# One weight load held for 1200 matmuls: the ones of a column sum kept in TensorE

## The chip, the cores and the metric

The kernel runs on one core of a Trainium2 chip. The metric is the device time of one execution in microseconds (us). The median of several is quoted. Single executions of one kernel here lie within about 0.4% (3 us) of each other, so differences under 1 us are read from several rounds and from the traces together. The engines are TensorE (matmuls; PE in the profile), VectorE (DVE), ScalarE (ACT), GpSimd (POOL) and SyncE (SP), which here issues the transfers. DMA engines, 16 of them, carry the transfers. A load *lands* when the last of them has reported its part.

## The reference, cut to what matters

```
x: (1, 384, 384, 384) bf16,  w1d: (1,) bf16
g = sum of x over the 384 x 384 positions, per channel, / (384 * 384)
s = sigmoid(g * w1d[0])                 # 384 numbers
return x * s                            # every position scaled by its channel
```

x has 113 MB. All of it must be summed before any of it can be scaled, and the kernels here keep only part of it on the chip, so most of it is read twice and all of it is written once: the page before has 190.41 MB read and 113.25 MB written.

## The kernel before

The 147456 positions are 1152 rows of 128 partitions x 384 channels. An arena on the chip holds 275 rows. In a first stage every row is read and summed by TensorE. Some rows stay in the arena for the second stage, and groups of them are squeezed by VectorE and ScalarE (`bits`, `join`, `test`: a fourth row is hidden in the spare bits of three others). In the second stage rows are scaled and stored, and the rest is read again.

The sum is a matmul with a 128 x 128 matrix of ones as weights and a row as moving data; all of them add into one bank `acc`:

```
def load(chunk, a, lo, hi):                       # one DMA from the queue of SyncE
    nc.sync.dma_start(out=arena[:, a : a + hi - lo, :], in_=view(xf, r0, n)[:, lo:hi, :])

def sum_rows(a, n):
    for i in range(a, a + n):                     # 1152 times in all
        nc.tensor.matmul(acc, lhsT=ones[:], rhs=arena[:, i, :], start=first, stop=last)   # L241

def keep_warm(n):                                 # 3 x 16 times, adds nothing
    nc.tensor.matmul(acc, lhsT=zeros[:], rhs=<ones, 384 columns>, start=False, stop=False)  # L256
...
# the last loads of the first stage: 13, 8, 13, 13, 8, 8, 5 and 3 rows
for a, n in S2 + [(U, 8)] + S3 + S1 + [(V, 8), (Y, 8), (T, 5), (T + 5, 3)]:
    take_raw(a, n)                                # load, then sum_rows
nc.scalar.activation(out=s_bf[:], in_=acc, func=ACTF.Sigmoid, scale=w_sc[:, 0:1])
...
# second stage: scale (VectorE), store and load (SyncE)
```

Each `matmul` becomes two instructions of TensorE, a weight load (LDWEIGHTS, in the profile "PEld") and the matmul proper ("PE").

Of the kernel before, what the change touches and what calls it, by code (L numbers as in the profile page):

```python
# [127 lines left out]
def kernel(  # L128
# [11 lines left out]
    nc = tc.nc  # L140
    P = nc.NUM_PARTITIONS
    B, H, W, C = x.shape
# [40 lines left out]
    ones = pool.tile([P, P], bf16, name="ones")  # L183
# [4 lines left out]
    arena = pool.tile([P, ROWS, C], bf16, name="arena")  # L188
    s_bf = pool.tile([P, C], bf16, name="s_bf")
    zeros = pool.tile([P, P], bf16, name="zeros")  # L190
    seen = pool.tile([P, 2 * len(pieces)], f32, name="seen")
    odd_i = pool.tile([P, 1], mybir.dt.int32, name="odd_i")
    bank0 = psum.tile([P, nc.PSUM_BANK_SIZE_BYTES // 4], f32, name="bank0")
    acc, votes = bank0[:, 0:C], bank0[:, C : C + 1]
# [12 lines left out]
    fl = Flow(nc, tc)  # L207
# [22 lines left out]
    def load(chunk, a, lo, hi):  # L230
# [5 lines left out]
            writes=rows(a, hi - lo), dma=True,  # L236
        )

    def sum_rows(a, n):
        def emit(i, first, last):  # L240
            return nc.tensor.matmul(acc, lhsT=ones[:], rhs=arena[:, i, :], start=first, stop=last)  # L241

        for i in range(a, a + n):
            first, last = summed[0] == 0, summed[0] == RPP - 1
            fl.add(
                "PE", lambda i=i, f=first, l=last: emit(i, f, l),
                reads=[("a", i), "ones"], writes=["bank0"],
            )
            summed[0] += 1

    def keep_warm(n):

        for _ in range(n):
            fl.add(
                "PE",
                lambda: nc.tensor.matmul(  # L256
                    acc, lhsT=zeros[:], rhs=ones[:, None, :].to_broadcast([P, C // P, P]), start=False, stop=False
                ),
                reads=["zeros", "ones"], writes=["bank0"],
            )  # L260

    def bits(dst, src, op0, s0, op1, s1, reads, writes):
        fl.add(
# [17 lines left out]
    def fold(k):  # L281
# [46 lines left out]
        reads=["ones", "w_bf"], writes=["bank0"],  # L328
# [4 lines left out]
        reads=["bank0"], writes=["w_sc"],  # L333
# [6 lines left out]
    def stream(n, a):  # L340
        load(STREAMED, a, streamed[0], streamed[0] + n)
        if n > 40 and folding:
            keep_warm(N_WARM)
        sum_rows(a, n)
        streamed[0] += n
# [11 lines left out]
    def take(g, lo=0, hi=None):  # L357

        a, q = GROUPS[g]
        hi = 4 * q if hi is None else hi  # L360
        load(KEPT, a + lo, c_group[g] + lo, c_group[g] + hi)
        sum_rows(a + lo, hi - lo)
# [36 lines left out]
    first = N_STREAM - between  # L399
# [22 lines left out]
    def take_raw(a, n):  # L422
        load(KEPT, a, raw(a), raw(a) + n)
        sum_rows(a, n)

    for a, n in S2 + [(U, 8)] + S3 + S1 + [(V, 8), (Y, 8), (T, 5), (T + 5, 3)]:
# [6 lines left out]
        reads=["bank0", "w_sc"], writes=["s_bf"],  # L433
# [231 lines left out]
    while True:  # L665

        if dve_at <= now:
# [4 lines left out]
            if landed and (ahead < PENDING or not can):  # L672
# [4 lines left out]
                if end or ahead < MERGE:  # L677
                    b, first = since
# [88 lines left out]
```

## Time and profile before

| kernel before | |
|---|---|
| median of the first 3 runs | 723.45 us |
| span of the profiled run | 721.3 us |
| TensorE | 1202 weight loads, 1202 matmuls, all but one in the first 270 us |
| landing of the last 8-row load that TensorE waits for | 266.50 us |

Three more lines of the page matter later: the first is from the part on busy time (engine, busy us, share, instructions), the others from the part on DMA queues (queue, kind: packets, MB, share of 16 engines).

```profile
PE 214.6 (30%) x1202; PEld 119.2 (17%) x1202; DVE 496.3 (69%) x470; ACT 115.4 (16%) x92; POOL 0.2 (0%) x4
...
q8 instruction: 9, 0.15, 0.1%
q14 instruction: 7, 0.06, 0.0%
```

Besides the data, the DMA engines fetch the engines' instructions: 9 packets on q8 and 7 on q14. By number, q8 is TensorE's. 9 packets of 16384 B over TensorE's 2404 instructions are 61 B for each (an estimate).

The timeline around 48 us (start us, us, engine, line, operation, count) shows how loads and matmuls lie:

```profile
47.83 1.46 PE L241 MATMUL bank<-arena,ones 128*128 128x384 bf16 x8
48.00 1.07 PEld L241 LDWEIGHTS bank<-arena,ones 128*128 128x128 bf16 x7
```

Seven loads lie inside eight matmuls that follow one another without a gap.

### The profile page before, as it was taken

What the parts mean: (1) busy time and instruction counts of PE and PEld (TensorE: products, weight loads), DVE (VectorE), ACT (ScalarE), POOL (GpSimd) and SP (SyncE); (2) the same over time, 40 slices, a digit from 0 to 9 for tenths busy, and PEclk for the clock granted to TensorE, in tenths of its full rate; (3) what the DMA queues carried; (4) which work ended last, traced back from release to release, by engine and by line L of the source; (5) the groups of instructions that cost most, each with busy time, mean ns of one, the idle gap of its engine ahead of it and who ended that gap; (6) DMA issues with size and microseconds to landing.
All of it is one profiled execution on the core that took longest, in us unless ns stands there. A gap on an engine that the chain in (4) does not pass through costs nothing.

```text
span 721.3 us, 3240 instructions
## 1 busy us (share of the span) xinstructions
PE 214.6 (30%) x1202; PEld 119.2 (17%) x1202; DVE 496.3 (69%) x470; ACT 115.4 (16%) x92; POOL 0.2 (0%) x4
## 2 busy tenths in 40 slices
PE   4677788897987770000000000000000000000000
PEld 2344445554543430000000000000000000000000
DVE  4600004788899819989799999999996992558500
ACT  3600003566677610002000000000000000000000
POOL 0000000000000000000000000000000000000000
PEclk9799999999899995555555555555555555555555
DMA  9999999999999978999999999999999999999997
GB/s 382 429 443 424 425 435 430 431 433 433 424 427 427 428 320 341 425 430 426 403 430 436 428 438 430 429 439 433 432 432 439 423 445 431 432 430 433 435 436 306
DMA packets 18882, 303.87 MB, mean 421 GB/s; under 512 B 2098, under 2 KB 2098, under 8 KB 4658
## 3 DMA queue, kind: packets, MB, share of 16 engines
q1 hardware_dynamic: 18864, 303.67, 98.6%
q8 instruction: 9, 0.15, 0.1%
q14 instruction: 7, 0.06, 0.0%
q10 hardware_dynamic: 2, 0.00, 0.0%
HBM read 190.41 MB, written 113.25 MB: 421 GB/s over the span
## 4 chain that ended last, share of the span: by engine, by line
DMA 55%; DVE 28%; PE 6%; ACT 5%; SPq 0%; issue 0%; another core or an unknown queue 0%; DVEq 0%
DMA arena<-in_x_dram 38%; DVE arena L441 19%; DMA out_dram<-arena 17%; DVE arena L265 6%; PE bank L241 6%; ACT arena L302 5%; DVE arena L271 3%; SPq L235 0%; ACT s_bf L432 0%; SPq L762 0%; DVEq L112 0%; SPq L106 0%
## 5 line engine op out<-in xcount | busy, mean ns | idle before, releaser
L441 DVE TENSOR_TENSOR arena<-arena,s_bf 128x1536 bf16<-128x1536 bf16 (+8 forms) x103 | 242.3, 2391 | 59.0 <-DMA arena<-in_x_dram 42.0
L265 DVE TENSOR_SCALAR arena<-arena 128x1536 uint16<-128x1536 uint16 (+2 forms) x247 | 145.5, 634 | 113.4 <-DMA arena<-in_x_dram 100.8
L241 PE MATMUL bank<-arena,ones 128*128 128x384 bf16 x1152 | 206.5, 341 | 52.7 <-DMA arena<-in_x_dram 52.6
L241 PEld LDWEIGHTS bank<-arena,ones 128*128 128x128 bf16 x1152 | 114.3, 102 | 144.6 <-DMA arena<-in_x_dram 58.7
L271 DVE TENSOR_TENSOR arena<-arena 128x1536 uint16<-128x1536 uint16 (+2 forms) x114 | 121.2, 1063 | 6.7 <-PE bank L241 4.4
L302 ACT ACTIVATE arena<-arena 128x3072 uint16<-128x3072 uint16 (+1 forms) x38 | 102.5, 2698 | 142.3 <-DVE arena L265 142.3
L514 PE MATMUL bank<-odd,ones 128*128 128x1 bf16 x1 | 0.2, 184 | 329.4 <-DVE odd L509 329.4
L514 PEld LDWEIGHTS bank<-odd,ones 128*128 128x128 bf16 x1 | 0.1, 103 | 329.8 <-DVE odd L509 329.8
L375 ACT COPY arena<-bank 128x512 uint32<-128x512 uint32 (+1 forms) x7 | 4.0, 571 | 61.8 <-DMA out_dram<-arena 61.6
L256 PE MATMUL bank<-ones,zeros 128*128 128x384 bf16 x48 | 8.3, 326 | 0.0
L302 ACT ACTIVATION_READ_ACCUMULATOR arena<-arena 128x1 f32 x38 | 7.1, 188 | 0.0
L256 PEld LDWEIGHTS bank<-ones,zeros 128*128 128x128 bf16 x48 | 4.7, 98 | 3.1
L375 ACT COPY bank<-arena 128x512 uint32<-128x512 uint32 (+1 forms) x7 | 3.6, 565 | 0.0
L432 ACT ACTIVATE s_bf<-bank,w_sc 128x384 bf16<-128x384 f32 x1 | 0.6, 581 | 15.4 <-PE bank L241 15.4
L735 ACT ACT_TABLE_LOAD x1 | 1.3, 1283 | 0.7 <-PEq L751 0.7
L332 DVE TENSOR_SCALAR w_sc<-bank 128x1 f32<-128x1 f32 x1 | 0.2, 159 | 1.1 <-PE bank L327 1.1
L322 DVE MEMSET ones<- 128x128 bf16 x1 | 0.2, 165 | 1.0 <-SPq L106 1.0
L327 PE MATMUL bank<-w_bf,ones 1*128 1x1 bf16 x1 | 0.2, 182 | 2.1 <-DMA w_bf<-in_w1d_dram 2.1
L327 PEld LDWEIGHTS bank<-w_bf,ones 1*128 1x128 bf16 x1 | 0.1, 100 | 2.1 <-DMA w_bf<-in_w1d_dram 2.1
L518 DVE CAST odd_i<-bank 128x1 int32<-128x1 f32 x1 | 0.2, 159 | 0.3 <-PE bank L514 0.3
L504 DVE TENSOR_REDUCE worst<-seen 128x1 f32<-128x38 f32 x1 | 0.2, 185 | 0.0
L509 DVE TENSOR_SCALAR odd<-worst 128x1 bf16<-128x1 f32 x1 | 0.2, 156 | 0.0
(5 smaller groups left out, 0.5 us busy)
## 6 DMA issues: line engine op xcount, KB each, us to landing
arena<-in_x_dram SPq DMA_DIRECT2D x15, 4608.0 KB, 33.9
arena<-in_x_dram SPq DMA_DIRECT2D x22, 1248.0 KB, 11.6
out_dram<-arena SPq DMA_DIRECT2D x8, 3072.0 KB, 30.3
arena<-in_x_dram SPq DMA_DIRECT2D x6, 3072.0 KB, 27.3
out_dram<-arena SPq DMA_DIRECT2D x12, 1248.0 KB, 11.8
out_dram<-arena SPq DMA_DIRECT2D x3, 4608.0 KB, 39.8
arena<-in_x_dram SPq DMA_DIRECT2D x3, 4512.0 KB, 37.9
out_dram<-arena SPq DMA_DIRECT2D x3, 4512.0 KB, 27.7
```

The costliest lines, as they stand in the source:

```text
L241: return nc.tensor.matmul(acc, lhsT=ones[:], rhs=arena[:, i, :], start=first, stop=last)
L256: lambda: nc.tensor.matmul(acc, lhsT=zeros[:], rhs=ones[:, None, :].to_broadcast([P, C // P, P]), start=False, stop=False),
L265: lambda: nc.vector.tensor_scalar(out=dst, in0=src, scalar1=s0, scalar2=s1, op0=op0, op1=op1),
L271: "DVE", lambda: nc.vector.tensor_tensor(out=dst, in0=a, in1=b, op=op), reads=reads, writes=writes
L302: lambda: nc.scalar.activation(out=y, in_=y, func=ACTF.Copy, accum_out=seen[:, 2 * k + i : 2 * k + i + 1]),
L322: fl.add("DVE", lambda: nc.vector.memset(ones[:], 1.0), writes=["ones"])
L327: lambda: nc.tensor.matmul(votes, lhsT=ones[0:1, :], rhs=w_bf[0:1, 0:1], start=True, stop=True),
L375: "ACT", lambda: nc.scalar.copy(dst.bitcast(u32), src.bitcast(u32)), reads=reads, writes=writes
L432: lambda: nc.scalar.activation(out=s_bf[:], in_=acc, func=ACTF.Sigmoid, scale=w_sc[:, 0:1]),
L441: lambda: nc.vector.tensor_tensor(out=v, in0=v, in1=s_bf[:, None, :].to_broadcast([P, n, C]), op=Op.mult),
L514: lambda: nc.tensor.matmul(votes, lhsT=ones[:], rhs=odd[:], start=True, stop=True),
L735: nc.scalar.preload_act_table(ACTF.Sigmoid)
```

## The change

The ones are loaded once, with the first sum. Every later matmul is issued without its weight load and uses what is held. The warm-keeping matmuls loaded zeros as weights; they now send zeros as moving data through the held ones, so that no other weights are loaded between two sums. The intent is to take 1199 weight loads off TensorE.

```
+    def add_held(rhs, stop=False):
+
+        pe = nc.tensor
+        return pe.add_instruction(
+            mybir.InstMatmult(
+                name=nc.get_next_instruction_name(),
+                ins=[pe.lower_ap(rhs), pe.lower_ap(ones[:])],
+                outs=[pe.lower_ap(acc)],
+                start_tensor_calc=False, stop_tensor_calc=stop,
+                tile_size=(P, P), tile_position=(0, 0), ldweights=False,
+            )
+        )
+
     def sum_rows(a, n):
         def emit(i, first, last):
-            return nc.tensor.matmul(acc, lhsT=ones[:], rhs=arena[:, i, :], start=first, stop=last)
+            if first:
+                return nc.tensor.matmul(acc, lhsT=ones[:], rhs=arena[:, i, :], start=first, stop=last)
+            return add_held(arena[:, i, :], last)
 ...
     def keep_warm(n):
 
         for _ in range(n):
-            fl.add(
-                "PE",
-                lambda: nc.tensor.matmul(
-                    acc, lhsT=zeros[:], rhs=ones[:, None, :].to_broadcast([P, C // P, P]), start=False, stop=False
-                ),
-                reads=["zeros", "ones"], writes=["bank0"],
-            )
+            fl.add("PE", lambda: add_held(zeros[:, None, :].to_broadcast([P, C // P, P])), reads=["zeros", "ones"], writes=["bank0"])
```

## The prediction

> **What bounds the kernel now.** I read the page from the top: slices, chain of waits, costliest groups. Then the chain in order of time, the timeline of TensorE (PE) alone, and a table of stretches for the two places where TensorE could matter.

> ```profile
> PE   4677788897987770000000000000000000000000
> PEclk9799999999899995555555555555555555555555
> DMA  9999999999999978999999999999999999999997
> DMA 55%; DVE 28%; PE 6%; ACT 5%; SPq 0%; issue 0%; another core or an unknown queue 0%; DVEq 0%
> L241 PE MATMUL bank<-arena,ones 128*128 128x384 bf16 x1152 | 206.5, 341 | 52.7 <-DMA arena<-in_x_dram 52.6
> L241 PEld LDWEIGHTS bank<-arena,ones 128*128 128x128 bf16 x1152 | 114.3, 102 | 144.6 <-DMA arena<-in_x_dram 58.7
> ```

> The first three lines cut the 721.3 us span into 40 slices of 18 us. TensorE works only in the first 15, where x is read and summed; the DMA row is 9 (90% or more) in every slice but two, the handover from summing to scaling, and the last. The fourth line is the chain that ended last: 6% of it is TensorE, 55% DMA. The last two are the groups that the change touches: 1152 matmuls and 1152 weight loads. TensorE's idle time before its matmuls (52.7 us) is nearly all for data to land (52.6 us): it is ahead of the transfers.

> By size: a row block of 128 partitions x 384 elements x 2 B is 98.3 KB. At the 423 to 436 GB/s that the stretches of the first stage show, it takes 0.225 to 0.232 us to arrive. TensorE's pace follows from its timeline (start us, us; the end of a stream is modelled, so its last matmul counts as a whole 326 ns):

> ```profile
> 44.73 7.97 PE L241 MATMUL bank<-arena,ones 128*128 128x384 bf16 x48 [2.46 <-DMA arena<-in_x_dram]
> 110.20 13.17 PE L241 MATMUL bank<-arena,ones 128*128 128x384 bf16 x80 [2.89 <-DMA arena<-in_x_dram]
> 180.73 28.02 PE L241 MATMUL bank<-arena,ones 128*128 128x384 bf16 x152 [3.01 <-DMA arena<-in_x_dram]
> ```

> (7.97 - 0.326) / 47 = 0.1626 us, and (13.17 - 0.326) / 79 = 0.1626 us: some 70% of the time in which a row arrives. The third line starts after a pause at half clock and catches up.

> Where TensorE does set the end is the handover:

> ```profile
> 254.26 12.24 DMA arena<-in_x_dram
> 266.50 0.05 issue
> 266.55 2.79 PE bank L241 x16
> 269.34 0.02 issue
> 269.36 0.59 ACT s_bf L432
> 269.95 0.02 issue
> 269.98 16.52 DVE arena L441 x9
> ```

> This is the chain in order of time. The last input lands at 266.5 us, 16 matmuls remain, then the sigmoid and the first scaling. Nothing can be stored before, and the arena is full of rows not yet summed or scaled, so the DMA is idle here (0.05 of it busy between 266.5 and 270 us, by the stretches). So what a change of TensorE is worth is read from these 2.79 us, 0.4% of the span, unless TensorE becomes slower than the transfers.

> [...] in the half-clock burst from 180.73 us the weight loads come every 0.32 us. [...] after 48.00 us, 7 loads lie inside 8 unbroken matmuls. [...] the granted clock is 0.52 in 180.7 to 187 us, after a 3.01 us pause, and 1.00 from 192 to 266.5 us. [...]

> **The change part by part.**

> *Removed: 1199 weight loads.* Every matmul of the sums but the first (1151) and all 48 warm-keeping ones lose theirs; three of 1202 loads stay (the weight of the attention, the first sum, the verdict), and the matmul with zeros reads zeros as moving data against the ones that are held. The order on each engine is otherwise the same as before, as is each transfer. By the group, 1199 x about 0.1 us = 119 us of load time go. But the spacing of matmuls is already 162.6 ns[...]. The 98 ns loads are entirely beside the matmul stream. Gain per matmul in a stream: about 0[...], in TensorE time that waits for data anyway.

> *On the path:* at the handover, 16 matmuls: (2.79 - 0.326) / 15 = 164 ns each[...]. The first matmul after a wait needs its own load; on the timeline load and matmul both start at 266.55 us or within 0.03 us, so removing it is worth 0.0 to 0.1 us. Sum: at most about 0.1 us.

> *Instruction fetch:* the queue of 0.15 MB of instructions fits TensorE's 2404 instructions[...]. Half goes: [...]at 421 GB/s 0.18 us of transfer, all of it in a stage that transfers bound. Gain 0.2 us at most, hidden in the noise.

> *Moved:* the waits for data stood before the loads; they now stand before the matmuls. No new wait, no buffer freed later. Sum of all: 723.45 - 0.1 - 0.15, so **723.2 us**.

> **The rivals.**

> *Clock lost.* [...] the clock may be halved more often. In the stage of small loads (209 to 266 us) the engine works in bursts of 2.29 us with pauses of 0.4 to 1.8 us at full clock; matmuls alone are busy 42.65 of 56.5 us there. At half clock a burst of 13 takes 13 x 0.32 = 4.2 us where the data of 13 rows takes 2.96 us: it falls behind, has no more pauses, and this should bring the clock back. What stays is perhaps 16 matmuls at 0.32 instead of 0.163 us, +2.5 us, and as much again for a backlog: 726 to 729 us. Only a clock that never rises would be worse: 1200 x 0.32 = 384 us of TensorE in place of 265 us, an end near 840 us. For it: the clock does fall after pauses of 2 to 4 us. Against it: matmuls stay as long and their pauses as short as before. I give the small loss about 0.08, the large one 0.01.

> *Transfers or vector work go faster without TensorE's weight reads.* 1199 reads of 32 KB are 39 MB less from the on-chip memory. Were that contention, the first stage would be slower than the second, where TensorE rests. It moves 436, 428 and 423 GB/s in the stretches 40 to 120, 120 to 180 and 192 to 266.5 us, against 430 in 300 to 580 us. At most 1% of some 265 us, 2.6 us, is open: 720.5 us. I give it 0.07.

> *Rows freed earlier, so loads start earlier.* The queue's own waits show SyncE waiting 169.1 us for TensorE to free rows before it issues loads. But the DMA share stays near 1.00 in all stretches up to 264 us, so loads queue behind others anyway. Expected gain 0; at most a few tenths of a microsecond.

> *The held path is itself slower,* say by a gap that each matmul without load pays. Up to 229 - 163 = 66 ns each it would be hidden but for the last 16 (1 us). I give it 0.03.

> **Range and chances.** The centre is 723.2 us. Runs of the kernel before spread 722.4 to 723.7 us, and another session may shift all by 0.3% (2 us). The clock rival draws the range up a little, the contention rival down: 720.8 to 725.8 us. A change of over 2% is 14.5 us, five times the whole chain piece of TensorE at the handover: faster 0.01, same 0.97, slower 0.02.

> **What would show it.** Right: the group of weight loads shrinks from 1152 to 1 and its busy time from 114.3 us to 0.1; the group of matmuls keeps 326 ns as its shortest, and a burst of 48 at full clock still takes 7.97 us; its idle time for landing data stays above 50 us; the handover still takes about 2.8 us from landing to sigmoid, and the last input lands at 266 to 267 us; the slices' DMA row looks the same. Wrong: a burst of 48 clearly under 7.9 us (loads did cost); a granted clock near 0.5 in slices that had 9, or a handover of 5 us (clock lost); over 440 GB/s throughout the first stage (contention); the last input landing some microseconds earlier. The total would be wrong only if one of the last three holds.

The sum above is 723.45 - 0.1 - 0.15 = 723.2 us. The 0.18 us of the fetch stand: half of the 0.15 MB on q8 at the page's 421 GB/s. That a stream without pauses brings the clock back is read from the burst at 180.73 us (granted clock 0.52 until 187 us, 1.00 from 192 us). That the clock falls after pauses holds for some of them: it was 0.50, 0.58 and 0.60 at the start of the bursts at 21.70, 32.62 and 66.57 us (pauses of 4.21, 1.99 and 2.99 us), but 1.00 in the one at 55.61 us, after 2.90 us. The 0.3% for another session was my guess; the medians of the kernel before were 723.45, 722.30 and 722.48 us.

## The result

The changed kernel took 721.85 us (median of 6 runs, 721.18 to 722.80), the kernel before 722.30 us (6 runs, 721.88 to 723.66). The ratio is 0.999, with a 95% interval of 0.9977 to 1.0003: the same. In this document a ratio is of mean times of runs in the same rounds, so not quite the ratio of the medians; in the experiments below it comes out of the listed times when the first, profiled run of each kernel is left out. The time is inside the predicted range, 1.35 us under its centre.

The page of the changed kernel, busy time, slices, chain by engine, groups and queues:

```profile
PE 213.6 (30%) x1202; PEld 0.3 (0%) x3; DVE 496.4 (69%) x470; ACT 115.4 (16%) x92; POOL 0.2 (0%) x4
...
PE   4678778897987770000000000000000000000000
...
PEclk9798999999999995555555555555555555555555
DMA  9999999999999979999999999999999999999996
...
q8 instruction: 4, 0.07, 0.0%
...
DMA 60%; DVE 27%; PE 4%; ACT 2%; SPq 0%; issue 0%; DVEq 0%; another core or an unknown queue 0%
...
L242 PE MATMUL bank<-arena,ones 128*128 128x384 bf16 x1151 | 205.2, 340 | 46.1 <-DMA arena<-in_x_dram 45.9
...
L255 PE MATMUL bank<-arena,ones 128*128 128x384 bf16 x1 | 0.5, 476 | 6.8 <-DMA arena<-in_x_dram 6.8
```

PEld fell from 119.2 us and 1202 loads to 0.3 us and 3. PE and its waits for data (45.9 + 6.8 = 52.7 us, before 52.6) are as they were, and its slices differ in single digits only. The instruction queue q8 moved 4 packets in place of 9.

The timeline of TensorE alone:

```profile
43.51 7.96 PE L242 MATMUL bank<-arena,ones 128*128 128x384 bf16 x48 [1.26 <-DMA arena<-in_x_dram]
109.89 13.16 PE L242 MATMUL bank<-arena,ones 128*128 128x384 bf16 x80 [2.92 <-DMA arena<-in_x_dram]
```

48 matmuls take 7.96 us, against 7.97; (7.96 - 0.326) / 47 = 0.1624 us each, against 0.1626. The stream is no faster. The chain in order of time at the handover:

```profile
254.31 11.31 DMA arena<-in_x_dram
265.62 0.04 issue
265.67 2.77 PE bank L242 x16
268.44 0.02 issue
268.46 0.59 ACT s_bf L442
269.06 0.02 issue
269.08 16.52 DVE arena L451 x9
```

TensorE's share of the handover is 2.77 us, before 2.79. But the load that it waits for landed at 265.62 us, before at 266.50: 0.88 us earlier, and the first scaling starts 0.90 us earlier. That is most of the 1.2 us between the two profiled spans (721.3 and 720.1 us). So the little that was gained came mainly from a transfer that landed sooner, though data, queue and order of the loads are unchanged.

**Where the 0.88 us are from.** The trace holds 16 landing times for each load, one for each of the 16 DMA engines as I read it, and for load 47 of the kernel before they lie up to 3.00 us apart. Worked out from them (first and last of the 16, and how many come over 0.8 us after the first), with the instruction packets that had started by the last landing, those before the span's start left out:

```
                  before                                     after
load    first    last    lag  late  q8+q14     first    last    lag  late  q8+q14
  4     32.13    32.57  0.44    0    0+0       32.01    32.56  0.55    0    0+0
  5     43.02    44.69  1.67    1    1+0       42.90    43.46  0.56    0    0+0
  6     53.91    55.56  1.65    1    1+0       53.78    55.49  1.71    1    1+0
  7     64.79    66.52  1.74    2    2+0       64.68    66.38  1.70    1    1+0
 13    126.49   128.27  1.78    4    4+0      126.38   128.13  1.75    2    2+0
 18    170.09   171.78  1.69    7    6+2      169.97   171.62  1.66    5    3+2
 30    218.04   220.21  2.16    8    7+3      217.98   220.27  2.29    6    4+3
 47    263.50   266.50  3.00    9    9+3      263.39   265.62  2.23    6    4+3
```

Until the first packet on q8 (36.1 us before, 48.2 us after) all 16 landings come within 0.6 us. From the next load on, one of the 16 is late by 1.1 to 1.2 us, and stays late. In the table most further packets on q8 come with another late engine (with q14's, 7 + 3 packets and 8 late engines at load 30 before, 4 + 3 and 6 after). The lateness was not made up while the queue was full: the largest lag stays between 1.62 and 1.85 us from load 6 to load 28 in both kernels. In the first transfer to land after the pause of the handover it is 0.16 and 0.17 us. A load counts as landed when its slowest engine is done (266.50 us for load 47 before, the last of its 16). The kernel before fetched 9 packets and one engine was hit twice (the packet at 252.1 us takes the lag from 2.0 to 3.1 us); the changed kernel fetched 4. There the slowest engine at the end was made late by packets of q14: at load 14, after the packet at 131.1 us, a third engine is late (by 1.51 us), and at load 29, after the one at 217.1 us, the largest lag goes from 1.67 to 2.42 us. That the ninth packet hit an engine already late is no chance: the lags of the narrow matmuls below show that TensorE's packets go around eight engines. Load 47 is the one that the handover waits for: its first landings differ by 0.11 us, its last ones by 0.88 us. Which engine a packet uses is not in the trace; that a packet holds up one engine is read from the lags.

### The profile page after: what moved, and what is told of

It is laid out like the page before. It is cut to its first block, busy times and chain, and to the rows that moved or that the text cites. A ratio compares the mean times of both kernels' runs of the same rounds, so it can differ in the third digit from the quotient of the medians.

```text
span 720.1 us, 2041 instructions
## 1 busy us (share of the span) xinstructions
PE 213.6 (30%) x1202; PEld 0.3 (0%) x3; DVE 496.4 (69%) x470; ACT 115.4 (16%) x92; POOL 0.2 (0%) x4
## 4 chain that ended last, share of the span: by engine, by line
DMA 60%; DVE 27%; PE 4%; ACT 2%; SPq 0%; issue 0%; DVEq 0%; another core or an unknown queue 0%
DMA arena<-in_x_dram 43%; DVE arena L451 19%; DMA out_dram<-arena 17%; DVE arena L275 5%; PE bank L242 4%; DVE arena L281 3%; ACT arena L312 2%; SPq L235 0%; ACT s_bf L442 0%; DVEq L112 0%; SPq L772 0%; SPq L112 0%; SPq L106 0%
## 5 line engine op out<-in xcount | busy, mean ns | idle before, releaser
L242 PE MATMUL bank<-arena,ones 128*128 128x384 bf16 x1151 | 205.2, 340 | 46.1 <-DMA arena<-in_x_dram 45.9
L242 PE MATMUL bank<-zeros,ones 128*128 128x384 bf16 x48 | 8.3, 326 | 0.0
L442 ACT ACTIVATE s_bf<-bank,w_sc 128x384 bf16<-128x384 f32 x1 | 0.6, 582 | 14.5 <-PE bank L242 14.5
L255 PEld LDWEIGHTS bank<-arena,ones 128*128 128x128 bf16 x1 | 0.1, 104 | 6.8 <-issue 6.8
```

The source lines that it names most:

```text
L242: return pe.add_instruction(mybir.InstMatmult(name=nc.get_next_instruction_name(), ins=[pe.lower_ap(rhs), pe.lower_ap(ones[:])], outs=[pe. ...
L255: return nc.tensor.matmul(acc, lhsT=ones[:], rhs=arena[:, i, :], start=first, stop=last)
L442: lambda: nc.scalar.activation(out=s_bf[:], in_=acc, func=ACTF.Sigmoid, scale=w_sc[:, 0:1]),
```

## The experiments

Theory: the weight loads were hidden beside the matmuls, and the gain comes from fewer instruction packets. Rivals: a weight load costs the matmul stream or the memory something; or the difference is noise. Eight kernels ran on one chip; all were correct. The kernel before had a median of 722.48 us there (9 to 10 runs).

### The changed kernel again

No edit.

> The changed kernel once more, unaltered, beside the kernel before in the same rounds. Theory of the fetches (the few tenths gained come from half as many instruction packets: 4 of 16384 B on the instruction queue in place of 9, each of which holds up one of the 16 DMA engines by about 1.2 us, so that the last loads of the first stage land 0.5 to 0.9 us earlier): ratio to the kernel before 0.9985 to 0.9995, the 8-row load next to last but two seen by TensorE at 265.6 to 265.9 us, against 266.55 us before. Theory of the loads (a weight load costs the matmul stream a little): the same ratio, but the landing does not move and the handover from landing to sigmoid is shorter by as much. Theory of noise: the ratio lies within 0.9995 to 1.0005.

Measured: 721.32 us (5 runs), ratio 0.9982 (0.9968 to 0.9996). The load before the handover landed at 265.57 us, and TensorE's part stayed 2.77 us. What moved is the landing, as the theory of the fetches has it; the ratio is a little under the 0.9985 that I had as the least. With both sessions, the gain is 0.1 to 0.2%, and only the second interval excludes a gain of zero; the slowest of the five runs (723.35 us, the profiled one) is not in it.

### The instructions put back, the loads not

```
+        if ones_added[0] <= 1160:        # counts the calls of add_held
+            <a held matmul of one column of zeros into acc[:, 0:1]>
         return pe.add_instruction(...)
```

> The changed kernel with as many TensorE instructions as before (in front of each of the first 1160 held matmuls a held matmul of one column of zeros, no weight load). Theory of the fetches: again 9 packets of 16384 B on the instruction queue, the last loads land as late as in the kernel before (seen at 266.2 to 266.8 us), ratio 0.9995 to 1.0005. Theory of the loads or of reads of weights: no weight is loaded, so all of the gain stays, ratio as that of the changed kernel in the same rounds (0.9985 to 0.9995) and the landing at 265.6 to 265.9 us. [...]

Measured: 722.58 us (5 runs), ratio 1.0004 (0.999 to 1.0017); 9 packets on q8 again. TensorE took 0.1875 us per row (16 rows from 40.00 to 43.00 us), 25 ns more than 162.6, less than the 229 ns in which a row arrives. The chain at the handover:

```profile
254.35 12.06 DMA arena<-in_x_dram
266.42 0.04 issue
266.46 2.77 PE bank L260 x16
```

The landing is back at 266.42 us (before 266.50), without one weight load more: 9 of the 16 engines were late at the end, as before. The gain left with the instruction count, and so it was not the loads' time nor their reads of memory. In time alone the two kernels' intervals still touch; the landing decides. Over all traces: with 4 packets on q8 started by then, load 47 landed at 265.22 to 265.62 us (four runs); with 9, at 266.42 and 266.50 us (two runs).

### Instructions of an idle engine

```
+    def idle_pool():
+        for _ in range(4800):
+            nc.gpsimd.drain(fusable=False)
+        return None
+
+    fl.add("POOL", idle_pool)
```

> The changed kernel with 4800 drain instructions on the idle GpSimd, which touch no data; [...]19 packets of 16384 B or 38 of 8192 B. Theory of the fetches: what counts is that a packet of instructions holds up one DMA engine, whosever instructions they are; more than one packet per engine, so every transfer of the first stage lands later: by 19 x 1.2 / 16 = 1.4 us if spread evenly, so 1 to 2.5 us more than the changed kernel, ratio to before 1.0005 to 1.003. Theory of the loads and theory of noise: as the changed kernel in the same rounds to within 0.05%.

Measured: 744.24 us (5 runs), ratio 1.0298 (1.0284 to 1.0312): slower by some 22 us. The direction was expected, the size was not: I had 1 to 2.5 us. (By the 9 packets for 2404 instructions of TensorE, 4800 make 18 of 16384 B or 36 of 8192 B, an estimate.) The page and the chain:

```profile
GB/s 373 433 439 436 422 431 434 428 431 351 403 421 283 352 362 200 391 428 433 412 427 434 430 434 429 441 429 434 437 420 445 428 431 439 431 432 434 434 435 295
...
q14 instruction: 44, 0.36, 0.1%
```

```profile
274.45 14.56 DMA arena<-in_x_dram
289.00 0.04 issue
289.05 1.48 PE bank L242 x8
```

There are 37 more packets on q14, of 8192 B. The 8-row load that had landed at 265.62 us landed at 286.98 us: 21.4 us later; 34 of the 37 had started by then, which makes 0.63 us each. The landing times say why it is so much. At load 13, 13 of the 16 engines are within 0.6 us, and one is late by 10.75 us; at load 18 it is 14.84 us. By these lags GpSimd's packets did not go around the engines as TensorE's do: they held up one and the same. Then loads that wait for freed rows are held up too, and in the tenth to sixteenth slice (167 to 297 us) the rate falls to between 200 and 421 GB/s (before, after the first slice, it was 424 to 443 GB/s up to the handover, and 320 and 341 in the two slices there). An engine that computes nothing cost 3% by its instructions alone.

### Sixteen matmuls more at the handover

```
+            if last:
+                for _ in range(16):
+                    add_held(zeros[:, None, :].to_broadcast([P, C // P, P]))
             return add_held(arena[:, i, :], last)
```

> The changed kernel with 16 more held matmuls of zeros just ahead of the very last sum. If the handover is where TensorE sets the end, all of 16 x 0.1626 = 2.6 us shows: the handover from the landing to the sigmoid grows from 2.77 to 5.4 us and the time by 2.2 to 3.0 us over the changed kernel (ratio to before 1.002 to 1.004). The rival, that TensorE is not on the path even there (the first scaling or the stores wait for something else): less than 1 us. This also tells what one nanosecond per matmul is worth: 16 ns of the total.

Measured: 724.51 us (5 runs), ratio 1.0032 (1.0018 to 1.0046), 3.2 us over the changed kernel by the medians and 2.3 us by the spans of the profiled runs (722.5 and 720.2).

```profile
265.48 0.04 issue
265.52 5.38 PE bank L242 x32
270.90 0.02 issue
```

The handover took 5.38 us in place of 2.77, 2.61 us for 16 matmuls. Here TensorE does set the end, so a nanosecond on every matmul would be worth some 16 ns of the total (an estimate from these 16).

### A second weight load for every matmul

```
+            if not first:
+                nc.tensor.ldweights(ones[:])
             return nc.tensor.matmul(acc, lhsT=ones[:], ...)      # the kernel before
```

> The kernel before with a second, redundant weight load of the ones in front of every matmul but the first: 3553 TensorE instructions, 14 instruction packets of 16384 B. If loads lie beside the matmuls and two in a row do not overlap each other, the pace becomes 2 x 98 = 196 ns per row (from 162.6), still under the 229 ns of the transfers, so only the last 16 rows show it (0.5 us), plus up to 0.6 us for five more packets: ratio to before 1.0005 to 1.002, a burst of 48 in 9.5 us. Rival: a load adds part of its time to the stream: if the second adds all of its 98 ns, 261 ns per row bind TensorE and the time grows by some 35 us.

Measured: 723.23 us (6 runs), ratio 1.0014 (1.0001 to 1.0026). Groups of weight loads, and a burst from the timeline:

```profile
L242 PEld LDWEIGHTS <-ones 128*128 128x128 bf16 x1151 | 117.2, 102 | 36.7
L243 PEld LDWEIGHTS bank<-arena,ones 128*128 128x128 bf16 x1152 | 109.7, 96 | 59.8 <-DMA arena<-in_x_dram 53.0 <-issue 6.8
```

```profile
44.61 7.97 PE L243 MATMUL bank<-arena,ones 128*128 128x384 bf16 x48 [1.22 <-DMA arena<-in_x_dram]
```

The burst of 48 still takes 7.97 us, where I had expected 9.5. Two loads whose records add up to 198 ns fit beside one matmul of 163 ns. The single loads show it:

```profile
48.04 0.10 PEld L242 LDWEIGHTS <-ones 128*128 128x128 bf16 x1
48.08 0.10 PEld L243 LDWEIGHTS bank<-arena,ones 128*128 128x128 bf16 x1
48.20 0.10 PEld L242 LDWEIGHTS <-ones 128*128 128x128 bf16 x1
48.24 0.10 PEld L243 LDWEIGHTS bank<-arena,ones 128*128 128x128 bf16 x1
```

Two start 0.04 us apart, each with a record of 0.10 us: the record of a load is longer than the time for which it keeps the next one out. The loads were hidden with more room than I had thought. Of 14 packets on q8, 13 had started by then, and load 47 did not land visibly later (266.53 us, with 9 packets 266.50); why, the next section shows. The 0.14% more in time is at the edge of its interval and stays unexplained.

### Narrow matmuls, with their loads

```
-   matmul(acc, lhsT=ones[:], rhs=arena[:, i, :], ...)            # cut; the very first row keeps this form
+   for c in (0, 128, 256):
+       matmul(acc[:, c : c + P], lhsT=ones[:], rhs=arena[:, i, c : c + P], ...)
```

> The kernel before with each row summed by three matmuls of 128 columns in place of one of 384, each with its own weight load. [...] If the pace is the load's, 3 x 98 = 294 ns per row exceed the 229 ns of the transfers, TensorE becomes the bound of the first stage: 1151 x 0.294 + 8 = 346 us in place of 266 us, some 80 us more, ratio 1.10 to 1.12. [...] If loads are free here too: ratio under 1.005.

Measured: 725.93 us (4 runs), ratio 1.0051 (1.0036 to 1.0067). This was a miss: not the 80 us of a pace set by the loads, and a little over the 1.005 that I had for free loads. I had expected that the loads could not hide (a third of 162.6 ns gives 54 ns for such a matmul, an estimate, against 98 ns for a load's record).

```profile
L243 PEld LDWEIGHTS bank<-arena,ones 128*128 128x128 bf16 x3453 | 203.0, 101 | 53.4 <-DMA arena<-in_x_dram 52.9 <-issue 0.2
```

```profile
212.11 2.18 PE L243 MATMUL bank<-arena,ones 128*128 128x128 bf16 x36 [0.38 <-DMA arena<-in_x_dram]
```

With the last matmul counted as a whole 0.22 us, (2.18 - 0.22) / 35 = 56.0 ns per matmul of 128 columns, each with a load of its own whose record is 101 ns. Even here the load is fully beside the matmul. So what cost 3.4 us? The page has 27 packets on q8, and the chain ends with another load, the last one, of 3 rows:

```profile
259.27 12.77 DMA arena<-in_x_dram
...
272.08 0.69 PE bank L243 x9
```

The sigmoid started at 272.80 us, before at 269.36: 3.44 us later, which is the loss. The lags of the 16 landings behind the first, in us and sorted, show how the packets did it (load 30, with 11 packets on q8 started in the runs with two loads and with narrow held matmuls, 22 here):

```
two loads     0.00 0.15 0.35 0.39 0.43 0.57 0.80 1.35 1.53 1.70 1.70 1.75 1.78 3.06 3.15 3.19
narrow, held  0.00 0.00 0.16 0.26 0.44 0.51 0.90 1.09 1.40 1.47 1.59 1.75 1.82 3.15 3.28 3.31
narrow, loads 0.00 0.01 0.01 0.19 0.29 0.32 0.57 1.23 3.04 3.21 4.16 4.35 4.45 4.55 4.60 4.79
```

By the lags, the 25th packet hit one engine for the fourth time. Load 41 landed 5.59 us after its first engine, at 255.03 us (before at 251.05), so its rows were freed later, and SyncE issued load 47 at 258.31 in place of 254.26 us. That is why even the first landing of load 47 was late (266.86 us in place of 263.50).

### Narrow matmuls, held

The same edit in the changed kernel.

> The changed kernel with each row summed by three held matmuls of 128 columns. [...] the transfers bind again: ratio to the kernel before 1.000 to 1.003 (14 instruction packets in place of 9, and some 0.1 us at the handover). With the run of narrow matmuls and loads beside it, this measures what the change is worth where the matmul is shorter than the load[...]. Rival: each matmul has a floor[...] (over 76 ns), then TensorE would bind here as well.

Measured: 723.31 us (4 runs), ratio 1.0015 (1.000 to 1.003), 13 packets on q8.

```profile
44.87 8.20 PE L242 MATMUL bank<-arena,ones 128*128 128x128 bf16 x144 [0.16 <-DMA arena<-in_x_dram]
```

(8.20 - 0.22) / 143 = 55.8 ns, as with loads. The two narrow kernels differ by 0.36% in their ratios with no difference in the pace of TensorE, but 13 packets against 27, and load 47 lands at 266.64 against 269.58 us. Holding the weights does pay here, by its fetches.

### Without the warm-keeping matmuls

`N_WARM = 0` in the changed kernel.

> The changed kernel without its 48 warm-keeping matmuls of zeros, to see whether the clock hangs on them: the rival of my prediction was a clock lost when TensorE has less to do. If the clock hangs on them, the bursts after 128, 146 and 164 us start at half clock and the first lands late, but the transfers hide it up to 66 ns a row: the ratio to before stays as that of the changed kernel, 0.997 to 1.000. If the clock were lost until the end of the stage, the handover would take some 5.4 us in place of 2.77 and the ratio rise to 1.002 or more.

Measured: 721.92 us (4 runs), ratio 0.9995 (0.998 to 1.0011).

```profile
128.22 14.58 PE L242 MATMUL bank<-arena,ones 128*128 128x384 bf16 x80 [3.51 <-DMA arena<-in_x_dram]
146.34 13.16 PE L242 MATMUL bank<-arena,ones 128*128 128x384 bf16 x80 [3.55 <-DMA arena<-in_x_dram]
```

The burst at 128 us starts slowly in the other two kernels as well (14.86 us before, 14.84 after; the granted clock from 128 to 132 us was 0.59 in both); the one at 146 us takes 13.16 us even after a pause of 3.55 us, as in the changed kernel, where the clock was 1.00 from 146.3 to 159 us. The clock of the handover does not hang on the 48 matmuls (TensorE's part is 2.77 us here too), nor on how often weights are loaded (2.79 us before, 2.77 after).

## Why the prediction was right, and what it had wrong

- **The total.** The range of 5 us is several times the effect, so the total by itself tests little; the lines below do. Of the 1.35 us under the centre, 1.15 are the starting number: 723.45 us, a median of three runs, was 722.30 us in six. The forecast gain was 0.25 us; measured were 0.45 us by the medians, 1.2 us by the profiled spans.
- **What bounds the kernel.** Right: the transfers bind the first stage; doubling the loads and narrowing the matmuls left it so. One reading was inexact. The chain's 266.5 us is not the landing of the last input but of the last 8-row load; the 5 and 3 rows after it landed at 267.63 and 268.33 us, while TensorE was summing. Its 16 matmuls ran without a gap all the same, and 16 more cost 2.61 us.
- **Loads removed from the stream: about 0.** Right: 0.2 ns each, by 7.97 and 7.96 us for 48. With two loads per matmul and with narrow matmuls it is shown, not only argued, that loads are beside the stream.
- **On the path at the handover: at most 0.1 us.** Right: 2.79 became 2.77 us.
- **Instruction fetch: half of 0.15 MB, 0.18 us, "0.2 us at most".** This is the term that was mis-sized. I spread the bytes over all 16 engines. By the lags, a packet of 16384 B holds up one of them and makes it some 1.2 us late, and the load lands with the slowest engine. It measured 0.88 us in the first pair of profiles and 0.93 us in the second (266.50 against 265.57 us). With it in place of the 0.15 us the sum would have been 723.45 - 0.1 - 0.9 = 722.5 us, not 723.2.
- **Rival: clock lost.** Did not happen: the granted clock is 1.00 from 192 to 266.5 us in both, and the slices differ in single digits only.
- **Rival: transfers faster without the reads of weights.** It had the right effect, an earlier landing, for a cause that does not hold: the one-column matmuls brought the late landing back without a single weight read.
- **Rivals: rows freed earlier, a slower held path.** Neither showed; the first landing of load 47 moved by 0.11 us, and the held stream is 0.2 ns per matmul quicker.
- **What would show it.** All signs of "right" came but one: the landing that I had expected at 266 to 267 us came at 265.6, and that was the sign of the missing term.

What stays open: which eight engines TensorE's packets go around, and why GpSimd's stayed on one; and whether a kernel with 8 packets would gain as much as this one with 4, as the steps of eight suggest. It was not run. No kernel here beats the changed one clearly.

## What to carry to other kernels

Before you remove weight loads, look in the timeline whether they lie inside matmuls that follow one another without a gap. Here they did (7 loads inside 8 matmuls), and the loads were hidden: the spacing was 162.6 ns with them and 162.4 ns without, and their 119 us of busy time were worth nothing in the stream. In a kernel that transfers bind, count instructions as transfers: here each packet of TensorE's made one DMA engine 1.1 to 1.2 us late, a load landed with its slowest engine, and the lateness stayed as long as the queue was full. So an unrolled stream, even on an idle engine, can cost more than the work in it (22 us for 37 packets on GpSimd).
